# Splitting float64 weights: a parametric ReLU with slope -2^32 on ScalarE in place of a scaled copy, and one VectorE operation fewer per chunk

## Chip, cores, metric

One Trainium2 chip, one core of it. The metric is the device time of one execution in microseconds (us), as the median of several runs. Engines: PE is TensorE (matmuls), ACT is ScalarE, DVE is VectorE, POOL is GpSimd, SP issues the DMAs.

## What is computed

A chunked state-space scan over 4 sequences of 768 tokens and 8 heads, followed by two feed-forward layers of 256 x 2048 x 256. The weights arrive as numpy's float64 (`np.random.randn(...) * factor`), cut here to what matters:

```python
# scan, per batch and head, chunks of 32 tokens (L = exp of cumulated log a, causal)
y[:, :, sl] = (CB * L) @ xc + (Cc @ state) * exp(cum)
state = exp(sum(la)) * state + sum_j Bc x xc * exp(cum[-1] - cum)
# layer 1 (weights moe_w_in, moe_w_out)
h = x @ w_in;  g = np.maximum(0.01 * h, h);  x = g @ w_out
# layer 2 (weights moe2_w_in, moe2_w_out)
h = np.maximum(x @ w_in, 0.0);  out = (h * h) @ w_out
```

## The kernel before

The 3072 tokens are 12 pieces of 256 tokens, three pieces per sequence. One piece goes through the scan in two halves, `scan_a` (scales, decays, the products S of `L389` and `L390`, then `mk`) and `scan_b` (`mkh` and `mkl`, the two halves of `mk`; products Y; states `stt`; `shl`, a transpose to `t16`, four copies or DMAs into `sbd`; the second products into Y; `yh` and `yl`, the scan's result as a high and a low float32r part, or `y32` for piece 0). Layer 1 follows in blocks of one or two pieces (class `One`: `hmm` makes `hp`, `act` makes `g`, `omm` adds into `oo` or `o`), layer 2 in groups of two pieces (class `Two`). Block 0 multiplies the float32 weights as they are (`L493`, `L526`); from piece 1 on every float32 operand is split into two float32r parts and multiplied three times (`L470` to `L472`).

A weight is read in 32 chunks of 128 x 512 numbers, eight of each matrix. A chunk is loaded as 64-bit integers (`load_w`, tile `wst`) and goes through three steps, each put between other work by hand-set rules (`raw_step`, `w_one`):

- `split_w`, on ACT: `L132` scales the high 32-bit words, read as float32, by 2^-112, which rebases the exponent; `L135` scales the low words, read as unsigned integers, down to their top three bits.
- `split_w1`, on DVE: `L143` shifts the high word left by 3 and ORs the low word's bits in, which loses the sign; `L148`, `L152` or `L156` (for layer 1, `w_in` of layer 2, `w_out` of layer 2) masks the sign bit out of the unshifted high word and ORs it in. For layer 1 the result is the tile `raw`.
- `split_w2`: ACT copies to a float32r high part (`L174`), DVE subtracts it (`L175`): tiles `w1i`, `w1o`, `w2i`, `w2o`.

The text is recorded as a program first; the tile framework then orders the instructions of each engine by its own estimate of their readiness. Each engine runs its list strictly in order. So the order is no fixed text: removing an instruction can move others. DMAs all leave from SP's queue, also in order. The buffers `wst` are seven, shared with other temporary tiles such as `all` (inputs of the next sequence, read by the sums of squares `sq` of `L274`).

ACT's table of functions is loaded once, at the start (`L84`).

Of the kernel before, what the change touches and what calls it, by code (L numbers as in the profile page):

```python
# [8 lines left out]
F32 = mybir.dt.float32  # L9
# [3 lines left out]
I32 = mybir.dt.int32  # L13
I64 = mybir.dt.int64
U32 = mybir.dt.uint32
AF = mybir.ActivationFunctionType
ALU = mybir.AluOpType
# [38 lines left out]
def ssd_moe_kernel(ctx: ExitStack, tc: tile.TileContext, in1, in2, w1i, w1o, w2i, w2o, out):  # L56
# [6 lines left out]
    nc = tc.nc  # L63
# [11 lines left out]
    def big(shape, dtype, name, tag="b", bufs=None):  # L75
        return heap.tile(shape, dtype, tag=tag, name=name, bufs=bufs)
# [3 lines left out]
    ones = cp.tile([P, P], F32, name="ones")  # L80
    nc.gpsimd.memset(ones, 1.0)
    pm = cp.tile([P, 1], F32, name="pm")
    lr = cp.tile([4, 1], F32, name="lr")
    nc.scalar.activation(lr, ones[0:4, 0:1], AF.Lrelu)  # L84
    delta = cp.tile([P, U, T], F16, name="delta")


# [38 lines left out]
    def split_w():  # L126
        nm, c, st = w_loaded.pop(0)
        v = st.bitcast(I32).rearrange("p k (f two) -> p k f two", two=2)
        w0, w1 = v[:, :, :, 0], v[:, :, :, 1]


        nc.scalar.activation(w1.bitcast(F32), w1.bitcast(F32), AF.Copy, scale=2.0**-112)  # L132


        nc.scalar.activation(  # L135
            w0, w0.bitcast(U32), AF.Copy, scale=2.0**-29 * (1 - 2.0**-14), bias=7.5 * 2.0**-14 - 0.5
        )
        w_half.append((nm, c, w0, w1))

    def split_w1():  # L140

        nm, c, w0, w1 = w_half.pop(0)
        nc.vector.scalar_tensor_tensor(w0, w1, 3, w0, ALU.logical_shift_left, ALU.bitwise_or)  # L143
        if nm[0] == "1":
            if c % 2 == 0:
                pair[nm] = big([P, 2, 2, 256], F32, "raw", *RAW[nm])
            w = w_raw[nm, c] = pair[nm][:, c % 2]
            nc.vector.scalar_tensor_tensor(w.bitcast(I32), w1, -(1 << 31), w0, ALU.bitwise_and, ALU.bitwise_or)  # L148
            w_full.append((nm, c, w))
            return  # L150
        if nm != "2o":
            nc.vector.scalar_tensor_tensor(w0, w1, -(1 << 31), w0, ALU.bitwise_and, ALU.bitwise_or)  # L152
            w_full.append((nm, c, w0.bitcast(F32)))
            return
        a = big([P, 8, P], F32, "wa", "st", 7)
        nc.vector.scalar_tensor_tensor(  # L156
            a[:, 0:4].rearrange("p (k d) f -> p k (d f)", k=2).bitcast(I32),
            w1, -(1 << 31), w0, ALU.bitwise_and, ALU.bitwise_or,
        )
        nc.vector.scalar_tensor_tensor(a[:, S1], a[:, 0], -1.0, a[:, A22], ALU.mult, ALU.subtract)  # L160
        nc.vector.tensor_tensor(a[:, S3], a[:, A11], a[:, 0], ALU.subtract)
        nc.vector.scalar_tensor_tensor(a[:, S2], a[:, S1], -1.0, a[:, A11], ALU.mult, ALU.subtract)
        nc.vector.tensor_tensor(a[:, S4], a[:, A12], a[:, S2], ALU.subtract)
        w_full.append((nm, c, a[:, 1:8]))
# [12 lines left out]
    def w_step():  # L177
        if w_full:
            split_w2()
        if w_half:  # L180
            split_w1()
        if w_loaded:
            split_w()
        if wq:
            load_w()

    def raw_step():
        if w_half:
            split_w1()
        if w_loaded:  # L190
            split_w()
        if wq[0][0][0] == "1":
            load_w()

    def w_one():

        if w_full:
            split_w2()
        elif w_half:
            split_w1()  # L200
        elif w_loaded:
            split_w()
        if wq and not w_loaded:
            load_w()
# [269 lines left out]
    class One:  # L474
# [22 lines left out]
        def act(self, ms):  # L497
            n, hp = self.n * TP, self.h
            if self.f32:
                g = big([P, 512], F32, "g32", "g", 3)  # L500
                nc.scalar.activation(g, hp, AF.Lrelu)
                for j, m in enumerate(ms):
                    self.g[m] = g[:, j * n : j * n + n]
                return
            t = ap_.tile([P, 512], F32, tag="t", name="t")
            g = big([P, 2, 512], F32R, "g", "g", 3)
            nc.scalar.activation(g[:, 0], hp, AF.Lrelu)  # L507
            nc.scalar.activation(t, hp, AF.Lrelu)  # L508
            nc.vector.tensor_tensor(g[:, 1], t, g[:, 0].bitcast(F32), ALU.subtract)  # L509
            for j, m in enumerate(ms):  # L510
                self.g[m] = g[:, 0, j * n : j * n + n], g[:, 1, j * n : j * n + n]
# [289 lines left out]
```

## Time and profile before

| what | value |
|---|---|
| median of 3 runs | 606.39 us (606.07 to 607.07) |
| the profiled execution | 606.45 us |
| its span, first to last instruction | 604.7 us |
| PE busy | 572.1 us, 95% |
| DVE busy | 455.6 us, 75%, 774 instructions |
| ACT busy | 445.5 us, 74%, 715 instructions |
| DMA moved | 46.50 MB, mean 77 GB/s |

The profiled execution is 1.75 us longer than its span: what lies before the first and behind the last instruction. An engine's busy share is an average; which engine is waited for in a stretch is read from the waits and from the rows in order of time.

### The profile page before, as it was taken

The numbers are of one execution on the slowest core, as the hardware profiler recorded it, in microseconds if no ns is written. First come the engines' busy times: TensorE is split into PE (matmuls) and PEld (weight loads), VectorE is DVE, ScalarE is ACT, GpSimd is POOL, SyncE is SP. The second block draws the span as 40 slices with busy tenths as digits, with TensorE's granted clock in tenths as the row PEclk, the third lists the DMA queues.
The fourth block names the chain that finished last, engine by engine and source line by source line (L and its number), as shares of the span: only waits on it lengthen the run. The fifth ranks groups of instructions, "written<-read, shape, count | busy, mean of one in ns | idle before, by whom it ended". The sixth has DMA issues, their size and how long they took to land.

```text
span 604.7 us, 11654 instructions
## 1 busy us (share of the span) xinstructions
PE 572.1 (95%) x4610; PEld 516.3 (85%) x4610; DVE 455.6 (75%) x774; ACT 445.5 (74%) x715; POOL 5.2 (1%) x15
## 2 busy tenths in 40 slices
PE   0399999999999999999999999999999999999996
PEld 0388899999999878888888889989999999999996
DVE  6999989569984979567655468787777877877765
ACT  6999876479676868556665588877878777777773
POOL 3000000000000000000000000000000000000000
PEclk9999999999999999999999999999999999999999
DMA  8864845573576663131210000010000100100101
GB/s 295 289 160 129 234 111 116 129 193 92 113 187 189 163 166 36 36 62 46 69 36 0 1 2 0 2 36 1 9 28 1 35 1 2 36 1 0 36 1 35
DMA packets 113574, 46.50 MB, mean 77 GB/s; under 512 B 94448, under 2 KB 103280, under 8 KB 113520
## 3 DMA queue, kind: packets, MB, share of 16 engines
q1 hardware_dynamic: 113520, 45.76, 28.3%
q8 instruction: 36, 0.59, 0.4%
q14 instruction: 18, 0.15, 0.1%
HBM read 36.83 MB, written 3.15 MB: 66 GB/s over the span
## 4 chain that ended last, share of the span: by engine, by line
PE 86%; DVE 7%; ACT 4%; issue 2%; DMA 1%; DVEq 0%; ACTq 0%
PE hp L470 13%; PE hp L471 13%; PE hp L472 13%; PE o L532 4%; PE o L611 4%; PE o L538 4%; PE o L533 4%; PE o L609 4%; PE o L610 4%; PE oo L533 3%; PE oo L538 3%; PE oo L532 3%; PE Ym L611 3%; PE Ym L610 3%; PE Ym L609 3%
## 5 line engine op out<-in xcount | busy, mean ns | idle before, releaser
L509 DVE TENSOR_TENSOR g<-t,g 128x512 fp32r<-128x512 f32 x88 | 60.5, 687 | 52.6 <-ACT t L508 52.4
L587 DVE TENSOR_TENSOR tl<-ts,th 128x1024 fp32r<-128x1024 f32 x48 | 58.8, 1226 | 47.1 <-ACT th L585 47.1
L507 ACT ACTIVATE g<-hp 128x512 fp32r<-128x512 f32 x88 | 52.3, 594 | 47.2 <-PE o L538 33.7
L470 PE MATMUL hp<-yl,w1i 128*128 128x256 f32 (+1 forms) x256 | 83.4, 326 | 0.7 <-DVE yl L449 0.7
L471 PE MATMUL hp<-yh,w1i 128*128 128x256 f32 (+1 forms) x256 | 83.2, 325 | 0.0
L472 PE MATMUL hp<-yh,w1i 128*128 128x256 f32 (+1 forms) x256 | 83.0, 324 | 0.0
L575 ACT ACTIVATE b<-hp 128x512 f32<-128x512 f32 x96 | 57.2, 596 | 33.0 <-PE hp L472 32.8
L470 PE MATMUL hp<-xl,w2i 128*128 128x512 f32 x192 | 75.4, 393 | 0.0
L471 PE MATMUL hp<-xh,w2i 128*128 128x512 f32 x192 | 75.3, 392 | 0.0
L472 PE MATMUL hp<-xh,w2i 128*128 128x512 f32 x192 | 74.8, 389 | 0.0
L585 ACT CAST th<-ts 128x1024 fp32r<-128x1024 f32 x48 | 50.3, 1047 | 16.8 <-DVE ts L584 16.8
L470 PEld LDWEIGHTS hp<-yl,w1i 128*128 128x128 f32 x256 | 48.7, 190 | 4.9 <-DVE yl L449 1.1
L508 ACT ACTIVATE t<-hp 128x512 f32<-128x512 f32 x88 | 52.2, 593 | 0.0
L472 PEld LDWEIGHTS hp<-yh,w1i 128*128 128x128 f32 x256 | 48.7, 190 | 3.7
L471 PEld LDWEIGHTS hp<-yh,w1i 128*128 128x128 f32 x256 | 48.7, 190 | 3.7
L576 ACT ACTIVATE b<-b 128x1024 f32<-128x1024 f32 x48 | 50.9, 1061 | 1.1
L586 DVE TENSOR_TENSOR bl<-b,bh 128x768 fp32r<-128x768 f32 x48 | 45.7, 952 | 0.0
L582 DVE TENSOR_TENSOR ts<-b 128x512 f32<-128x512 f32 x48 | 33.2, 691 | 14.5 <-ACT b L576 13.5
L472 PEld LDWEIGHTS hp<-xh,w2i 128*128 128x128 f32 x192 | 36.1, 188 | 7.8
L470 PEld LDWEIGHTS hp<-xl,w2i 128*128 128x128 f32 x192 | 36.2, 189 | 6.3
L471 PEld LDWEIGHTS hp<-xh,w2i 128*128 128x128 f32 x192 | 36.2, 189 | 5.8
L581 ACT CAST bh<-b 128x768 fp32r<-128x768 f32 x48 | 40.1, 835 | 1.3
(167 smaller groups left out, 1571.4 us busy)
## 6 DMA issues: line engine op xcount, KB each, us to landing
in<-in SPq DMA_DIRECT2D x12, 640.0 KB, 4.9
in<-in SPq DMA_DIRECT2D x12, 512.0 KB, 5.7
all<-in SPq DMA_DIRECT2D x15, 384.0 KB, 4.3
wst<-w1i SPq DMA_DIRECT2D x8, 512.0 KB, 6.6
wst<-w1o SPq DMA_DIRECT2D x8, 512.0 KB, 6.4
wst<-w2i SPq DMA_DIRECT2D x8, 512.0 KB, 7.4
wst<-w2o SPq DMA_DIRECT2D x8, 512.0 KB, 4.2
out_t<-r SPq DMA_DIRECT2D x24, 128.0 KB, 1.7
```

What stands on the lines that cost most here:

```text
L470: nc.tensor.matmul(hp, wh[:, k, c], xl[:, :, k], start=(k == 0), stop=False)
L471: nc.tensor.matmul(hp, wh[:, k, c], xh[:, :, k], start=False, stop=False)
L472: nc.tensor.matmul(hp, wl[:, k, c], xh[:, :, k], start=False, stop=(k == KI - 1))
L507: nc.scalar.activation(g[:, 0], hp, AF.Lrelu)
L508: nc.scalar.activation(t, hp, AF.Lrelu)
L509: nc.vector.tensor_tensor(g[:, 1], t, g[:, 0].bitcast(F32), ALU.subtract)
L532: nc.tensor.matmul(self.o[d], wl[:, c], gh, start=(m == 0 and (d == 0 or self.n == 2)), stop=False, **kw)
L575: nc.scalar.activation(b[:, 2 * i : 2 * i + 2], hp.rearrange("p (n t) -> p n t", n=2), AF.Relu)
L576: nc.scalar.activation(b, b, AF.Square)
L585: nc.scalar.copy(th, t)
L586: nc.vector.tensor_tensor(bl, b[:, 1:], bh.bitcast(F32), ALU.subtract)
L587: nc.vector.tensor_tensor(tl, t, th.bitcast(F32), ALU.subtract)
```

## The change

ACT's operation on the high word becomes a parametric ReLU: a positive word is scaled by 2^-112 as before; a negative one is scaled and multiplied by -2^32 too. That makes it positive and raises its exponent by 32, which is bit 28 of the word; DVE's shift by 3 then brings that bit to place 31, the sign. So the mask operation goes, and the shift writes where the mask operation wrote. Layer 1's leaky ReLU is written as the parametric one with slope 0.01, so that it stays one function on ACT.

```diff
-    nc.scalar.activation(lr, ones[0:4, 0:1], AF.Lrelu)
+    nc.scalar.activation(lr, ones[0:4, 0:1], AF.Prelu, alpha=0.01)
...
-        nc.scalar.activation(w1.bitcast(F32), w1.bitcast(F32), AF.Copy, scale=2.0**-112)
+        nc.scalar.activation(w1.bitcast(F32), w1.bitcast(F32), AF.Prelu, scale=2.0**-112, alpha=-(2.0**32))
...
         nm, c, w0, w1 = w_half.pop(0)
-        nc.vector.scalar_tensor_tensor(w0, w1, 3, w0, ALU.logical_shift_left, ALU.bitwise_or)
         if nm[0] == "1":
...
-            nc.vector.scalar_tensor_tensor(w.bitcast(I32), w1, -(1 << 31), w0, ALU.bitwise_and, ALU.bitwise_or)
+            nc.vector.scalar_tensor_tensor(w.bitcast(I32), w1, 3, w0, ALU.logical_shift_left, ALU.bitwise_or)
...
-            nc.vector.scalar_tensor_tensor(w0, w1, -(1 << 31), w0, ALU.bitwise_and, ALU.bitwise_or)
+            nc.vector.scalar_tensor_tensor(w0, w1, 3, w0, ALU.logical_shift_left, ALU.bitwise_or)
...
-            w1, -(1 << 31), w0, ALU.bitwise_and, ALU.bitwise_or,
+            w1, 3, w0, ALU.logical_shift_left, ALU.bitwise_or,
...
-                nc.scalar.activation(g, hp, AF.Lrelu)
+                nc.scalar.activation(g, hp, AF.Prelu, alpha=0.01)
...
-            nc.scalar.activation(g[:, 0], hp, AF.Lrelu)
-            nc.scalar.activation(t, hp, AF.Lrelu)
+            nc.scalar.activation(g[:, 0], hp, AF.Prelu, alpha=0.01)
+            nc.scalar.activation(t, hp, AF.Prelu, alpha=0.01)
```

The changed text is one line shorter, so behind this place the same instruction has a line number lower by one (`L410` before is `L409` after). The built programs show three places where the order moved. In the rows a name's number tells buffers apart.

First, DVE between piece 0's `mkl` and its states `stt`. Before:

```order
L410 TENSOR_TENSOR mkl_186<-in2_111,mkh_185 128x768
L225 TENSOR_SCALAR d1e_94<-in2_164 128x16
L226 TENSOR_SCALAR in2_164<-in2_164 128x16x31
L227 MEMSET in2_164 128x16
L143 SCALAR_TENSOR_TENSOR wst_116<-wst_116 128x512
L230 SCALAR_TENSOR_TENSOR le_371<-in2_164,delta_89 128x512
L148 SCALAR_TENSOR_TENSOR raw_382<-wst_116 128x512
L337 TENSOR_SCALAR eb_339<-S_337 128x3
L143 SCALAR_TENSOR_TENSOR wst_118<-wst_118 128x512
L252 SCALAR_TENSOR_TENSOR stt_285<-dec0_95,d1s_228 128x288
```

and after:

```order
L409 TENSOR_TENSOR mkl_186<-in2_111,mkh_185 128x768
L226 MEMSET in2_164 128x16
L147 SCALAR_TENSOR_TENSOR raw_381<-wst_116 128x512
L229 SCALAR_TENSOR_TENSOR le_371<-in2_164,delta_89 128x512
L234 SCALAR_TENSOR_TENSOR le_371<-in2_164,d1e_94 128x512
L336 TENSOR_SCALAR eb_339<-S_337 128x3
L147 SCALAR_TENSOR_TENSOR raw_392<-wst_118 128x512
L251 SCALAR_TENSOR_TENSOR stt_285<-dec0_95,d1s_228 128x288
```

Of three weight operations two are left, each now writing `raw` at once; piece 1's second scan `L234` has come ahead of `stt`, and `L224` and `L225` stand ahead of `mkl`.

Second, DVE between piece 1's `mk` and its low half `mkl`. Before:

```order
L399 SCALAR_TENSOR_TENSOR in2_164<-S_454,kk_358,le_371 128x16x32
L148 SCALAR_TENSOR_TENSOR raw_636<-wst_418 128x512
L225 TENSOR_SCALAR d1e_94<-in2_374 128x16
L337 TENSOR_SCALAR eb_653<-S_649 128x3
L226 TENSOR_SCALAR in2_374<-in2_374 128x16x31
L338 TENSOR_SCALAR eb_653<-eb_653 128x3
L227 MEMSET in2_374 128x16
L143 SCALAR_TENSOR_TENSOR wst_425<-wst_425 128x512
L410 TENSOR_TENSOR mkl_453<-in2_164,mkh_452 128x768
```

and after:

```order
L398 SCALAR_TENSOR_TENSOR in2_164<-S_447,kk_358,le_371 128x16x32
L174 TENSOR_TENSOR w1i_710<-raw_381,w1i_710 128x512
L336 TENSOR_SCALAR eb_642<-S_638 128x3
L229 SCALAR_TENSOR_TENSOR le_676<-in2_374,delta_89 128x512
L337 TENSOR_SCALAR eb_642<-eb_642 128x3
L234 SCALAR_TENSOR_TENSOR le_676<-in2_374,d1e_94 128x512
L409 TENSOR_TENSOR mkl_446<-in2_164,mkh_445 128x768
```

Both scans of piece 2 (`L229`, `L234`) now stand ahead of piece 1's `mkl`; before, both stood behind it.

Third, ACT around piece 1's `yh`. Before:

```order
L174 ACTIVATE w1o_1152<-raw_557 128x512
L174 ACTIVATE w1i_1204<-raw_636 128x512
L448 ACTIVATE yh_615<-Y_502,fac_360 128x512
L274 ACTIVATE sq_689,mx_626<-all_682 128x768
L411 ACTIVATE qh_848<-le_687,sc_654 128x512
```

and after:

```order
L173 ACTIVATE w1i_1188<-raw_625 128x512
L173 ACTIVATE w1o_1191<-raw_703 128x512
L273 ACTIVATE sq_678,mx_617<-all_671 128x768
L447 ACTIVATE yh_606<-Y_495,fac_360 128x512
L410 ACTIVATE qh_832<-le_676,sc_643 128x512
```

The sum of squares `sq`, whose input `all_671` a DMA brings, has changed places with `yh`. Its DMA stands on SP behind the four DMAs into `sbd` in both programs.

## Rows read from the trace of the kernel before

**Rows 1.** The page's first part, busy us (share of the span) and instructions of TensorE.

```profile
PE 572.1 (95%) x4610; PEld 516.3 (85%) x4610; DVE 455.6 (75%) x774; ACT 445.5 (74%) x715; POOL 5.2 (1%) x15
```

**Rows 2.** Waits of TensorE: engine, line, waited for: us in total, times, longest.

```profile
PE Y L419 <- DVE mkl L410: 1.4, 2, 1.0
PE o L532 <- DVE yf L547: 1.3, 1, 1.3
PE oo L526 <- DVE raw L148: 0.9, 1, 0.9
PE hp L470 <- DVE yl L449: 0.7, 1, 0.7
```

**Rows 3.** Groups by line: busy us, mean ns | idle before, releaser.

```profile
L507 ACT ACTIVATE g<-hp 128x512 fp32r<-128x512 f32 x88 | 52.3, 594 | 47.2 <-PE o L538 33.7 <-PE hp L472 13.2
...
L132 ACT ACTIVATE wst<-wst 128x512 f32<-128x512 f32 x32 | 21.7, 679 | 3.2 <-DMA wst<-w2o 3.2
L143 DVE SCALAR_TENSOR_TENSOR wst<-wst 128x512 int32<-128x512 int32 x32 | 21.7, 686 | 2.6 <-ACT wst L135 2.5
...
L365 ACT ACTIVATE him<-in,sbp 128x512 f16<-128x512 f32 x12 | 8.7, 722 | 0.3 <-DVE sbp L344 0.2
...
L84 ACT ACT_TABLE_LOAD x1 | 1.3, 1283 | 0.7 <-PEq L791 0.7
```

**Rows 4.** VectorE in order of time, 18 to 38 us: start, us, instruction.

```profile
18.68 0.95 DVE L410 TENSOR_TENSOR mkl<-in,mkh 128x768 f16<-128x768 f32 x1
...
20.57 1.22 DVE L230 TENSOR_TENSOR_SCAN le<-in,delta 128x512 f32<-128x512 f32 x1
...
25.12 0.70 DVE L431 STREAM_TRANSPOSE t<-shl 128x512 f16<-128x512 f16 x1
...
37.08 1.29 DVE L143 SCALAR_TENSOR_TENSOR wst<-wst 128x512 int32<-128x512 int32 x2
```

**Rows 5.** ScalarE in order of time, 26 to 35 us.

```profile
26.00 1.24 ACT L355 COPY sbd<-t 32x512 f16<-32x512 f16 x2
...
29.01 0.45 ACT L444 ACTIVATE y<-Y,fac 128x256 f32<-128x256 f32 x1
...
34.19 0.60 ACT L501 ACTIVATE g<-hp 128x512 f32<-128x512 f32 x1 [1.02 <-PE hp L493]
```

**Rows 6.** TensorE in order of time, 29 to 64 us; idle before it in brackets.

```profile
29.52 8.21 PE L493 MATMUL hp<-y,raw 128*128 128x256 f32 x24 [1.16 <-ACT y L444]
...
46.55 0.19 PE L419 MATMUL Y<-mkl,xbh 128*128 128x48 f16 x1
...
58.45 1.10 PE L526 MATMUL oo<-g,raw 128*128 128x256 f32 x4 [0.88 <-DVE raw L148]
60.20 2.41 PE L526 MATMUL oo<-g,raw 128*128 128x256 f32 x10
63.31 0.39 PE L470 MATMUL hp<-yl,w1i 128*128 128x256 f32 x1 [0.71 <-DVE yl L449]
```

**Rows 7.** VectorE in order of time, 42 to 63 us.

```profile
42.44 0.75 DVE L399 SCALAR_TENSOR_TENSOR in<-S,kk,le 128x512 f32<-128x512 f32 x1 [0.40 <-PE S L390]
...
45.03 0.95 DVE L410 TENSOR_TENSOR mkl<-in,mkh 128x768 f16<-128x768 f32 x1
...
54.01 0.71 DVE L431 STREAM_TRANSPOSE t<-shl 128x512 f16<-128x512 f16 x1
...
62.51 0.75 DVE L449 SCALAR_TENSOR_TENSOR yl<-Y,fac,yh 128x512 fp32r<-128x512 f32 x1
```

**Rows 8.** In order of time, SP's queue at 57 us and ScalarE at 61 to 63 us.

```profile
57.50 0.56 SPq L315 DMA_DIRECT2D all<-in  x1
...
61.81 0.67 ACT L448 ACTIVATE yh<-Y,fac 128x512 fp32r<-128x512 f32 x1
62.38 0.83 ACT L274 ACTIVATE sq<-all 128x768 bf16<-128x768 f32 x1
```

**Rows 9.** From issue to landing of that DMA of 384 KB (line 315, at 57.5 us).

```profile
DMA to landing us min/median/max: 4.3/4.3/4.3
```

## The prediction

> **What bounds the kernel now.** I read the busy shares first: TensorE is busy for 572.1 of 604.7 us, VectorE for 75% and ScalarE for 74% [rows 1]. So a saving on VectorE counts only where TensorE waits for it. The second view is the list of TensorE's waits [rows 2]. Behind its dense work's start only four remain: 0.9 us for `raw`, 0.7 us for `yl`, 1.3 us for `yf`, and the shorter of the two waits for `mkl`, 1.4 - 1.0 = 0.4 us; 3.3 us together. The third view is each engine in order of time. Dense work starts at 29.52 us, when ScalarE's `y` is there [rows 5, 6]; the waits for `raw` and `yl` follow at 58.45 and 63.31 [rows 6]. Up to there VectorE and ScalarE run almost without a gap, feeding piece 0, piece 1 and the first weights. So the head of 63 us decides, and in it one question: when does TensorE get each thing it needs, in the new order?
>
> **The change, part by part.** *What goes:* 32 VectorE operations of 686 ns, 21.7 us, at the price of the equal form `L143` [rows 3]. Nearly all of it lies beside TensorE's work; the most that this can give are the 3.3 us of waits and an earlier start.
>
> *What is exchanged on ScalarE:* 32 scaled copies of 679 ns and 184 leaky ReLUs (88 + 88 + 8) of 594 ns become parametric ReLUs. No row shows one. From below I take no saving, since the operand sizes stay; from above the price of an operation that fetches a per-partition operand, 722 ns, so at most 0.04 us on the scaling and 0.13 us on a leaky ReLU [rows 3]. I take 0: both kinds are single passes with constants, nearest to the rows they replace.
>
> Were the parametric ReLU in another function table than the copies and squares around it, each scaling would need two loads of 1283 ns [rows 3]: 64 x 1.28 = 82 us, and the time 688 us. The built program has one load, at the start, as before; so I give this no chance.
>
> The Trainium skill, "ScalarE: Activation LUTs", section "What ACT_TABLE_LOAD costs", prices such a switch at about 2.66 us with the drain that goes with it; by that the 64 would cost 170 us (an estimate from that page). No run here shows a switch between functions.
>
> *What moves:* times below are start to start; on VectorE one 512-wide operation follows another after 0.60 us (two take 1.29, one 0.69) and a scan occupies 1.22 - 0.09 = 1.13 [rows 4]. The order is the second thing that the change alters, and I walk down it.
>
> Term 1, the start. `mkl` of piece 0 can start some 0.2 us before 18.68, when its other half `mkh` is ready. Behind it now come one `raw` (which must wait for ScalarE until 19.6), two scans and another `raw`, then `stt`: 19.63 + 0.60 + 2 x 1.13 + 0.07 + 0.60 = 23.16, 0.2 later than before. Between `stt` and the transpose stands a further `raw`, and the transpose starts at 25.44 instead of 25.12 [rows 4]. It also stands behind `L224` on piece 2's input; that DMA is asked for when `mkl` ends, 19.4, and with 4.3 us for 384 KB [rows 9], so 5.7 for its 512 KB, lands at 25.1, in time. ScalarE's share of the copies into `sbd` starts at 26.4 instead of 26.00, behind `him` and `ch`, and its `y` follows 3.0 us later as before (two copies and three operations stand between): 29.4 instead of 29.01 [rows 5]. Start of dense work: **+0.38 us**.
>
> Term 2, `mkl` of piece 1. ScalarE's first `g` slips with the start, 34.19 to 34.57, and then works without a gap through `qh`, seven weight operations, a `g` and three sums of squares, 7.2 us by their durations less 0.1 each; VectorE waits for the last weight, writes its `raw` and can start `mk` at 42.47 (42.44 before, so level). Before, `mkl` came 45.03 - 42.44 = 2.59 us later. Now stand ahead of it `mk` 0.67, `w1i` 0.60, two scans 2.26 and two small ones 0.14: 3.67, so 46.14, end 47.09 [rows 7]. TensorE comes to `L419` at 46.55 + 0.38, less one `L526` that is now behind it (two records; six more of them take 2.41 - 1.10, so 0.44): 46.49 [rows 6]. It waits until 47.15. **+0.65 us**. Queued behind this wait are `L526` and the rest of piece 1's products, so all of TensorE is late by 1.03.
>
> Term 3, the wait of 0.88 for `raw` at 58.45. VectorE's last `raw` but two now lies at 55.1 to 55.7; TensorE arrives at 58.6. The wait goes: **-0.88**.
>
> Term 4, `yl` of piece 1. From 42.47 VectorE runs through 24 more operations, 8.9 us by the same spacings, to piece 1's `stt` at 51.34, and its transpose ends at 55.05 (before 54.01 + 0.71 = 54.72) [rows 7]. SP then issues four copies and the DMA for `all`, which left 2.78 us after the transpose's end before: 57.83; it lands 4.3 us later, at 62.13 [rows 8, 9]. ScalarE would be there at 61.3 and stands before it. `sq` takes 0.82, so `yh` starts at 63.0, not 61.81; `yl` 0.70 later and TensorE 0.80 after that, as in the rows of before: 64.5 [rows 6 to 8]. TensorE is ready at 63.31 - 0.71 - 0.88 + 1.03 + 0.44 = 63.19 (one more `L526` is done by then). The wait is 1.3 instead of 0.71: **+0.60**.
>
> Term 5, the later waits for `mkl` (0.4) and `yf` (1.3). The rows between TensorE's last product and these waits are the same in number on ScalarE; on VectorE a transpose replaces a mask operation in front of `yf`. I take +0.1; both ends are small, from -0.3 (the lighter VectorE) to +0.3. Behind 215 us TensorE did not wait for VectorE for more than 0.1 us, so the rest of the saving is covered by matmuls; without that cover it would be worth up to 0.6 us a chunk.
>
> Sum: 0.38 + 0.65 - 0.88 + 0.60 + 0.1 = **+0.85 us**. Against the profiled execution that is 606.45 + 0.85 = 607.3; that execution is 0.06 above the median of the runs, so I say **607.2 us**, 0.13% above before. A change of 0.2%, 1.2 us, is about what a measurement of this kernel can tell from none.
>
> **The rivals.**
> *No net loss.* Where `all` lands before ScalarE's 61.3, term 4 falls to 0.0 or below: `yh` at 62.1, TensorE at 63.6, wait 0.4. For it: 4.3 is one landing, and the DMA engines are idle ahead of it. Against: SP sends it only after the transpose. Time: 606.3 to 606.5.
> *Faster.* The start is not late and `yl` is no longer last: if VectorE's lighter load lets the transposes of pieces 0 and 1 come early, the waits of 0.88 and 0.71 go and terms 1 and 2 are 0. It decides where `yl` ends before TensorE's 62.2. For it: sixteen VectorE operations fewer in the head, 9.6 us at 0.60. Against: the freed places are filled with scans and splits ahead of what TensorE wants. Time: 606.4 - 1.6 = 604.8.
> *A dearer parametric ReLU.* At the upper ends of the bound, seven scalings ahead of `y` cost 7 x 0.04 = 0.3; three scalings and two `g` behind that 0.1 and 0.3; then yh's queue another 0.5 at most. For it: ScalarE has no gap in the head. Against: in the blocks it idles 47 us before `g` [rows 3], so the 176 there are covered. Time: 607.2 + 1.2 = 608.4.
>
> **How the numbers follow.** Forecast 0.52, with its own range 606.6 to 607.9 (each of terms 1, 2, 4 may be off by 0.3); no net loss 0.22; faster 0.10; dearer 0.16. Below 605.2 lies the faster case: 0.10. Above 607.6 lie the dearer one and 0.3 of the forecast's: 0.16 + 0.16 = 0.32. Between: 0.58. The range from 605.7 to 608.2 leaves out the faster case and the upper part of the dearer one.
>
> **What would show it.** Dense work starting at 29.9 and not 29.5; a new wait of TensorE for `mkl` near 47 us of some 0.6; no wait for `raw` near 58; the wait for `yl` near 64 grown, with `sq` in front of `yh` released by a DMA; the `yf` wait near 212 still there. A parametric ReLU at other than 0.68 us (scaling) or 0.59 (from PSUM) would make the sum wrong, as would a DMA that lands ahead of 61.3, or a new wait in the blocks, of which the trace of before has no sign.

## The result and the profile after

The changed kernel takes 609.87 us (median of 4 runs, 609.39 to 609.95), the kernel before 606.58 us in the same session: ratio 1.0053, 95% interval 1.0035 to 1.0070, so 3.3 us slower. The forecast was 607.2 us, with a range up to 608.2. The profiled execution took 609.87 us, its span is 608.1.

The busy line of the page and the row of granted clock, 40 slices of 15.2 us; below them the row of granted clock of the kernel before (slices of 15.1 us):

```profile
PE 574.0 (94%) x4610; PEld 517.7 (85%) x4610; DVE 438.0 (72%) x742; ACT 445.8 (73%) x715; POOL 5.2 (1%) x15
...
PEclk9999899999999999999999999999999999999999
```

```profile
PEclk9999999999999999999999999999999999999999
```

VectorE lost the 32 operations and 17.6 us, ScalarE kept its time to 0.3 us [rows 1]. What is new is the 8 in the fifth slice, 61 to 76 us: TensorE did not have its full clock there.

TensorE's waits (engine, line, what it waited for: us in total, times, longest):

```profile
PE hp L469 <- DVE yl L448: 2.1, 1, 2.1
PE o L531 <- DVE yf L546: 1.3, 1, 1.3
...
PE Y L418 <- DVE mkl L409: 1.0, 2, 0.6
```

The wait for `raw` has gone, the waits for `mkl` are 0.61 and 0.35 us, `yf` is unchanged, and the wait for `yl` has grown from 0.7 to 2.1 us [rows 2]. TensorE in order of time shows where each lies, and what follows the long one:

```profile
29.89 8.36 PE L492 MATMUL hp<-y,raw 128*128 128x256 f32 x24 [1.11 <-ACT y L443]
...
47.42 0.18 PE L418 MATMUL Y<-mkl,xbh 128*128 128x48 f16 x1 [0.61 <-DVE mkl L409]
...
65.35 0.39 PE L469 MATMUL hp<-yl,w1i 128*128 128x256 f32 x1 [2.14 <-DVE yl L448]
65.57 0.28 PE L470 MATMUL hp<-yh,w1i 128*128 128x256 f32 x1
65.69 0.29 PE L471 MATMUL hp<-yh,w1i 128*128 128x256 f32 x1
...
66.93 0.41 PE L471 MATMUL hp<-yh,w1i 128*128 128x256 f32 x1
67.14 0.41 PE L469 MATMUL hp<-yl,w1i 128*128 128x256 f32 x1
67.36 0.41 PE L470 MATMUL hp<-yh,w1i 128*128 128x256 f32 x1
```

Up to 66.4 us these matmuls begin 0.12 us apart. From 66.7 to 69.7 us the same matmuls begin 0.21 us apart, with nothing to wait for. The stretches (length; PE, PEld, DVE, ACT, POOL busy; granted clock; DMA share; GB/s) say why:

```profile
64.00:66.00 2.00, 0.65 (x5) 0.65 (x6) 1.46 (x3) 2.00 (x4) 0.00 (x0) 1.00 0.95 162
66.00:68.00 2.00, 2.00 (x14) 2.00 (x14) 1.16 (x5) 1.76 (x5) 0.00 (x0) 0.64 0.12 20
68.00:70.00 2.00, 2.00 (x10) 2.00 (x10) 2.00 (x4) 0.53 (x2) 0.00 (x0) 0.51 0.93 284
70.00:72.00 2.00, 2.00 (x39) 1.75 (x38) 1.02 (x2) 1.91 (x4) 0.00 (x0) 1.00 0.97 167
```

After the idle 2.14 us the granted clock is at its lower level, 1.2 of 2.4 GHz, for (0.36 + 0.49) x 2 / 0.5 = 3.4 us. The next wait, for `mkl`, is equally long in both kernels; after and before:

```profile
98.65 0.18 PE L418 MATMUL Y<-mkl,xbh 128*128 128x48 f16 x1 [0.35 <-DVE mkl L409]
```

```profile
95.33 0.18 PE L419 MATMUL Y<-mkl,xbh 128*128 128x48 f16 x1 [0.35 <-DVE mkl L410]
```

From the matmul that waited for `yl` to this one pass 98.65 - 65.35 = 33.30 us; before, 95.33 - 63.31 = 32.02 [rows 6], with one `L526` of 0.44 more to do in it. So the half clock cost 33.30 - 32.02 + 0.44 = 1.7 us. The Trainium skill, "TensorE: Matmul & The Clock Gate", section "Terms", prices a throttled time at its length times the share of the clock that is missing: 3.4 x 0.5 = 1.7; the trace agrees.

Why `yl` is late stands on ScalarE and SP's queue, in order of time:

```profile
58.09 0.57 SPq L314 DMA_DIRECT2D all<-in  x1
...
61.02 0.64 ACT L173 ACTIVATE w1o<-raw 128x512 fp32r<-128x512 f32 x1
63.00 0.84 ACT L273 ACTIVATE sq<-all 128x768 bf16<-128x768 f32 x1 [1.34 <-DMA all<-in]
63.75 0.19 ACT L273 ACTIVATION_READ_ACCUMULATOR sq<-all 128x1 f32 x1
63.84 0.67 ACT L447 ACTIVATE yh<-Y,fac 128x512 fp32r<-128x512 f32 x1
```

`sq` stands ahead of `yh`, and ScalarE is idle for 1.34 us until the DMA of `all` has landed; before, `yh` ran at 61.81 and `sq` behind it [rows 8]. That DMA left at 58.09 us. By the list of DMA issues (KB each, us to landing) it took 4.8:

```profile
all<-in SPq DMA_DIRECT2D x1, 384.0 KB, 4.8
```

The groups by line show the price of the new operation (busy us, mean ns | idle before, what ended it):

```profile
L506 ACT ACTIVATE g<-hp 128x512 fp32r<-128x512 f32 x88 | 52.4, 595 | 48.8 <-PE o L537 34.1 <-PE hp L471 14.5
...
L132 ACT ACTIVATE wst<-wst 128x512 f32<-128x512 f32 x32 | 21.6, 674 | 3.3 <-DVE wa L162 1.7 <-DMA wst<-w2o 1.6
```

595 and 674 ns, against 594 and 679 [rows 3]. My theory A: the loss is the late `yl` (+1.4 us) and the half clock behind its wait (+1.7 us), the other terms cancelling. Against it stand B, the parametric ReLU costs something that the means hide, and C, the new order loses in many places.

### The profile page after: what moved, and what is told of

It reads as the page before. It is cut to its first block, busy times and chain, and to the rows that moved or that the text cites. A ratio compares the mean times of both kernels' runs of the same rounds, so it can differ in the third digit from the quotient of the medians.

```text
span 608.1 us, 11627 instructions
## 1 busy us (share of the span) xinstructions
PE 574.0 (94%) x4610; PEld 517.7 (85%) x4610; DVE 438.0 (72%) x742; ACT 445.8 (73%) x715; POOL 5.2 (1%) x15
## 4 chain that ended last, share of the span: by engine, by line
PE 84%; ACT 7%; DMA 3%; DVE 3%; issue 1%; SPq 1%; DVEq 0%; ACTq 0%
PE hp L469 13%; PE hp L470 13%; PE hp L471 13%; PE o L531 4%; PE o L610 4%; PE o L537 4%; PE o L532 4%; PE o L608 4%; PE o L609 4%; PE oo L531 3%; PE oo L537 3%; PE oo L532 3%; PE Ym L610 3%; PE Ym L609 3%; PE Ym L608 3%
## 5 line engine op out<-in xcount | busy, mean ns | idle before, releaser
L471 PEld LDWEIGHTS hp<-yh,w1i 128*128 128x128 f32 x256 | 49.4, 193 | 3.8
L470 PEld LDWEIGHTS hp<-yh,w1i 128*128 128x128 f32 x256 | 49.4, 193 | 3.7
```

Of the source, the lines that this page charges most:

```text
L470: nc.tensor.matmul(hp, wh[:, k, c], xh[:, :, k], start=False, stop=False)
L471: nc.tensor.matmul(hp, wl[:, k, c], xh[:, :, k], start=False, stop=(k == KI - 1))
```

## The experiments

Times are medians; a kernel is compared with the kernel before of the same session (606.11 us in the first two, 606.23 in the third). An edge is an order given to the framework by hand: what stands inside the `with` may not be issued ahead of the named instruction. A record is one instruction's entry in the trace. The last column is the lowest granted clock in any 2 us of that stretch.

| kernel | us | ratio to before, 95% interval | wait for `yl` | least clock, 62 to 72 us |
|---|---|---|---|---|
| before with the new operation alone | 605.78 | 0.9997, 0.9988 to 1.0006 | 0.74 | 1.00 |
| changed, `yh` ahead of `sq` | 606.46 | 1.0005, 0.9996 to 1.0014 | 0.73 | 1.00 |
| before, `yh` twice | 605.99 | 0.9996, 0.9987 to 1.0005 | 0.72 | 1.00 |
| changed, two edges on scans | 605.17 | 0.9990, 0.9981 to 0.9998 | 0.55 | 1.00 |
| before, `yh` five times | 609.08 | 1.0052, 1.0037 to 1.0067 | 3.71 | 0.50 |
| changed, ten useless matmuls | 610.34 | 1.0066, 1.0049 to 1.0083 | none | 1.00 |
| changed, `all` loaded earlier | 605.67 | 0.9998, 0.9978 to 1.0018 | 0.62 | 1.00 |
| changed, three edges | 605.95 | 1.0001, 0.9992 to 1.0010 | 1.10 | 1.00 |
| changed, seven useless matmuls | 609.86 | 1.0049, 1.0032 to 1.0065 | 0.39 | 1.00 |
| changed, `all` earlier, two edges | 605.32 | 0.9980, 0.9968 to 0.9992 | 0.89 | 1.00 |
| before, `all` loaded earlier | 606.32 | 1.0002, 0.9984 to 1.0019 | 0.64 | 1.00 |

### The operation alone

The sign operation stays, and the order of every engine is that of before. So that the shift does not bring a sign along, negative high words get slope 1. The leaky ReLUs are parametric ones with slope 0.01.

```diff
-        nc.scalar.activation(w1.bitcast(F32), w1.bitcast(F32), AF.Copy, scale=2.0**-112)
+        nc.scalar.activation(w1.bitcast(F32), w1.bitcast(F32), AF.Prelu, scale=2.0**-112, alpha=1.0)
...
```

> The kernel before with its weights' shift and its leaky ReLUs done as parametric ReLU, VectorE's sign operation kept, and every engine's order as before. Theory A (the loss of the change comes from piece 1's late `yl` and from the half clock that follows its wait): the instruction costs nothing, 606.6 us, with 95.3-like waits as before and the granted clock at 1.00 from 60 to 75 us. Theory B (parametric ReLU is dearer, in itself or by a table): 608 to 610 us, and a mean above 690 ns for the 128x512 shift.

605.78 us, and the scaling's mean is 681 ns. B is out: the operation costs nothing here.

### The changed kernel with `yh` ahead of `sq`

```diff
-            squares(mx[:, to : to + 1], t)
+            with tc.issue_after(last["yh", 1].ins) if s == 1 and to == 3 else nullcontext():
+                squares(mx[:, to : to + 1], t)
...
-        nc.scalar.activation(yh, Y[:, :, 0:T], AF.Copy, scale=fac)
+        last["yh", p] = nc.scalar.activation(yh, Y[:, :, 0:T], AF.Copy, scale=fac)
```

> The changed kernel with one edge more: the squares of piece 1 may not be issued ahead of `yh` of piece 1, so that ScalarE makes `yh` before `sq`, which waits for a DMA. TensorE's order is that of the changed kernel. Theory A: the wait of 2.1 us for `yl` shrinks to 0.4 to 0.7 us, the granted clock stays at 1.00 from 60 to 75 us, and the time falls by 1.5 + 1.7 = 3.2 us to about 606.6 us. Theory B (instruction price) and theory C (the loss is spread over the reordered program): 608 to 610 us. If the wait is the whole loss without the clock: 608.3 us.

606.46 us: level with before. TensorE executes the changed kernel's list. ScalarE makes `qh` and `yh` ahead of `sq` here, and on VectorE `ql` and one `w1o` have changed places with their neighbours; the rest is the same. Its wait for `yl`, from the list of TensorE's waits:

```profile
PE hp L470 <- DVE yl L449: 0.7, 1, 0.7
```

And its stretches in which the changed kernel had a clock of 0.64 and 0.51:

```profile
66.00:68.00 2.00, 2.00 (x35) 1.75 (x34) 1.76 (x3) 1.15 (x3) 0.00 (x0) 1.00 1.12 326
68.00:70.00 2.00, 2.00 (x26) 1.95 (x23) 1.75 (x3) 1.77 (x4) 0.00 (x0) 1.00 0.56 64
```

So `sq` ahead of `yh` on ScalarE held the whole loss, and C is out. It does not yet tell the wait's own 1.4 us from the clock's 1.7.

### The wait put into the kernel before, twice

```diff
+        for _ in range(1 if p == 1 else 0):
+            nc.scalar.activation(yh, Y[:, :, 0:T], AF.Copy, scale=fac)
         nc.scalar.activation(yh, Y[:, :, 0:T], AF.Copy, scale=fac)
```

> The kernel before, without any of the change, with `yh` of piece 1 made twice on ScalarE (the same operation, the same result), which puts it and `yl` behind `sq` and the DMA that `sq` waits for. Theory A: TensorE waits about 2.1 us for `yl` near 63 us instead of 0.7, the granted clock then falls to 0.5 for about 3.4 us, and the time is 606.6 + 1.4 + 1.7 = 609.7 us. If the wait does not bring the clock down: 608.0 us. Theories B and C (price of the instruction, or the new order elsewhere): at most 608.0 us, since neither is in this kernel.

605.99 us, a miss. The product that needs `yl` came 1.75 us later, as wanted, but the scheduler had seen that coming and put eight more `oo` records of 0.216 us in front; TensorE in order of time:

```profile
60.20 4.13 PE L528 MATMUL oo<-g,raw 128*128 128x256 f32 x18
65.06 0.39 PE L472 MATMUL hp<-yl,w1i 128*128 128x256 f32 x1 [0.72 <-DVE yl L451]
```

So a late `yl` costs nothing while TensorE has other work ahead of it; the test of the clock had to use that work up. The same edit with 4 for 1:

> The kernel before, without any of the change, with `yh` of piece 1 made five times on ScalarE (the same operation and result each time), so that `yl` comes about 4 us later. TensorE has five more `oo` matmuls (1.1 us) to put ahead of `yl`, and then nothing: the planned order puts a wait of 2.2 to 2.8 us there. Theory A1 (a wait of 2 us or more there brings the granted clock down for some 3 us): 0.5 in the rows of about 66 to 70 us, and 606.1 + (2.5 - 0.7) + 1.7 = 609.6 us. Theory A2 (the wait costs its own length alone): 607.9 us, clock 1.00.

609.08 us, 3.0 over before, with none of the change in it. The wait came out at 3.71 us, longer than planned, so the time alone does not decide: 3.0 us more of wait at its length alone would give 609.1 too. But the later waits and the slow first matmuls (last section) take 2.1 us less in this trace than before, which leaves room for the clock, and the clock fell, by stretches:

```profile
64.00:66.00 2.00, 0.00 (x0) 0.00 (x0) 1.45 (x5) 2.00 (x5) 0.00 (x0) 1.00 0.30 29
66.00:68.00 2.00, 0.47 (x2) 0.50 (x3) 2.00 (x5) 2.00 (x5) 0.00 (x0) 0.80 0.97 331
68.00:70.00 2.00, 2.00 (x38) 1.91 (x37) 1.54 (x3) 1.36 (x4) 0.00 (x0) 0.50 0.99 132
70.00:72.00 2.00, 2.00 (x17) 2.00 (x16) 2.00 (x3) 0.81 (x2) 0.00 (x0) 0.85 0.24 26
```

The fall of the clock belongs to the wait, not to the change.

### The wait filled with work of no use

The output does not change: the added products go into a bank of TensorE's output memory that the next matmul clears.

```diff
+            if self.p0 == 1 and ms[0] == 0:
+                for _ in range(10):
+                    nc.tensor.matmul(self.h[:, 0:TP], w_raw["1i", 0][:, 0, 0:P], y32[:, 0], start=True, stop=True)
```

> The changed kernel with ten matmuls of no use (into the `hp` bank that the next one clears) ahead of the matmul that waits for `yl`: 10 x 0.216 = 2.2 us of TensorE. ScalarE's order is the changed kernel's, so `yl` is as late; four `oo` matmuls (0.9 us) move behind. TensorE then waits 2.14 - 2.16 + 0.86 = 0.84 us. Theory A1: the clock stays at 1.00, and against the changed kernel's +3.3 us the time is +3.3 - 1.3 (idle) + 2.2 (useless work) - 1.7 (clock) = 2.5 us over the kernel before, 608.6 us. Theory A2 or C (the half clock has another cause): 0.5 again after 66 us, and +4.2 us, 610.3 us.

I had taken one such matmul for one record; it is two, so ten were 4.3 us and left no wait. 610.34 us is the time that I had given the theory with another cause, but the half clock that it needs did not come: the granted clock stayed at 1.00. With 2.2 us more work than planned the time says little by itself. With seven:

> As the kernel with ten useless matmuls, with seven. Each one of them is two records of 0.216 us in the trace (so ten were 4.3 us and left no wait at all): seven are 3.0 us, and four `oo` matmuls (1.7 us) move behind. TensorE then waits 2.14 - 3.02 + 1.73 = 0.85 us for `yl`, about as long as the kernel before does. Theory A1: clock 1.00 from 60 to 75 us, and over the kernel before 3.3 - 1.3 + 3.0 - 1.7 = 3.3 us, plus up to 1 us of later waits as with ten: 609.4 to 610.4 us. Theory A2 (the half clock is not the wait's): 0.5 in the rows after 66 us, 611 us or more.

609.86 us. ScalarE still has `sq` ahead of `yh`, but TensorE's list of waits has only this for `yl`:

```profile
PE hp L469 <- DVE yl L448: 0.4, 1, 0.4
```

And its clock stays up, by stretches:

```profile
66.00:68.00 2.00, 2.00 (x23) 1.70 (x22) 2.00 (x6) 1.27 (x3) 0.00 (x0) 1.00 0.91 281
68.00:70.00 2.00, 2.00 (x38) 2.00 (x35) 1.97 (x4) 1.48 (x3) 0.00 (x0) 1.00 0.98 168
```

Against the changed kernel's trace the last wait (0.12 us, for layer 2) comes 0.8 us earlier, at 601.07 for 601.87 us, though TensorE does 3.0 us more. The other differences are 1.75 less of this wait, 0.2 less of the waits behind it, a start 0.2 later and three slow matmuls fewer at the start, 0.6 (last section): +0.6 without the clock, -1.1 with its 1.7 us. -0.8 is close to the second. So 3.0 us of useless work cost next to nothing, since it kept the clock up: each in its own session, 3.6 us over before with it and 3.3 without.

All thirteen traces agree on the price of the clock. From the end of TensorE's last matmul I take the start of the dense work, TensorE's waits from there on, what the slow first matmuls take beyond 0.216 us each, and the useless work, all from its rows in order of time. What is left is 564.4 us in the kernel before and 564.1 to 564.8 in the ten other traces in which the clock stayed up; it is 566.15 in the changed kernel and 565.9 with `yh` five times, 1.7 and 1.5 more than before.

### The transfer asked for earlier

```diff
-        for to, at in ((0, N + T), (3, N + T + 16), (1, N), (4, N + 16), (2, 0)):
...
+        def load_all(at):
             t = big([P, NPC, U * 16], F32, "all", "st", 7)
             nc.sync.dma_start(t, all_[:, :, U * at : U * (at + 16)])
+            ld.append(t)
...
+        load_all(ats[0][1])
+        for i, (to, _) in enumerate(ats):
+            if i < 4:
+                load_all(ats[i + 1][1])
             yield
-            squares(mx[:, to : to + 1], t)
+            squares(mx[:, to : to + 1], ld[i])
```

> The changed kernel with each of the five loads of `all` issued one step earlier (one load ahead of the squares that need it). No edge is put on ScalarE, but the plan then has `yh` of piece 1 ahead of the `sq` behind it. Theory A: `sq` no longer holds up `yh`; the wait for `yl` is 0.4 to 0.9 us, the clock 1.00 from 60 to 75 us, 606 to 607 us. Theory C (the loss is spread over the reordered program): 608 us or more.

605.67 us: the loss is gone here too, with the framework's planned order itself putting `yh` first; one of the ten runs took 610.8 us all the same (last section). And the same edit on the kernel before:

> Control: the kernel before, sign operation and all, with the loads of `all` one step earlier. Theory A: nothing waits for these loads in the kernel before in front of `yl` (`yh` stands ahead of `sq`), so the time is that of before, 606.1 us, within 0.5 us. If the early loads are a gain of their own, with or without the change: 605.5 us or less.

606.32 us. The early load is no gain of its own; it only undoes the changed kernel's defect.

### Orders that might beat both

First, piece 2's scans behind piece 1's `mkl`, and piece 1's start scan behind piece 0's `stt`:

```diff
+        with tc.issue_after(last["mkl", 1].ins) if p == 2 else nullcontext():
             lt, e1 = decays(az)
...
+        with tc.issue_after(last["stt", 0].ins) if p == 1 else nullcontext():
             from_start(p, az, e1)
```

> The changed kernel with two edges more: the scans of piece 2 come behind `mkl` of piece 1, and piece 1's start behind piece 0's `stt`; in the order that results ScalarE also makes `yh` of piece 1 ahead of `sq`. Theory A: the later start (+0.4) and the wait near 47 us (+0.6) go, the wait for `raw` (0.9) stays away, the wait for `yl` is 0.4 to 0.7 us and the granted clock stays at 1.00 from 60 to 75 us: about 605.5 us. Theory B: 608 us or more. Theory C (the reordered program loses elsewhere): 607 us or more.

605.17 us, 0.9 under before. The wait for `mkl` near 47 us went, but the dense work started at 30.97 us: the scan, let go behind `stt`, still stood ahead of the `sbd` chain. With the edge on the `sbd` copies instead, and `yh` ahead of `sq`:

> The changed kernel with three edges: piece 1's start scan behind piece 0's `sbd` copies, piece 2's scans behind piece 1's `mkl`, and the squares of the second sequence behind `yh` of piece 1. Theory A with the terms of the forecast: the dense work starts near 28.9 us (0.6 ahead of before, since `stt` and the `sbd` chain have VectorE to themselves), no wait near 47 us, no wait for `raw` (0.9), the wait for `yl` at 0.4 to 0.7 us: 606.1 - 1.5 = 604.6 us. If the gain of the removed sign operations is lost elsewhere: 606 us.

605.95 us, no gain. The start came at 29.20 us and the waits for `raw` near 58 us and for `mkl` near 47 us went, as asked, but the wait for `yl` grew to 1.10: `yl` ended no earlier than before, so part of what was saved ahead of it was waited out there. Part of the earlier start was lost at once, too. The third weight load of TensorE (PEld) had to wait for VectorE's half of `y`, which the same view of the kernel before does not show:

```profile
30.50 0.50 PEld L496 LDWEIGHTS hp<-y,raw 128*128 128x128 f32 x2 [0.79 <-DVE y L448]
```

Last, the two edges with the early load:

> The changed kernel with the loads of `all` one step earlier and two edges (piece 1's start scan behind piece 0's `sbd` copies, piece 2's scans behind piece 1's `mkl`). If the terms of the forecast add up: start at 29.2 us, no wait near 47 us and none for `raw`, 0.6 us for `yl`: 605.2 us, at best with the kernel that has only the two scans moved. If what is saved ahead of `yl` is given back in the wait for it (as in the kernel with three edges): 606.0 us.

605.32 us, 0.9 us under the kernel before, as with the first two edges. Its ratio of 0.9980 (0.9968 to 0.9992) looks better than theirs because three of the runs of the kernel before that it is compared with took over 608 us (last section). From its list of TensorE's waits:

```profile
PE hp L504 <- ACT y L455: 1.1, 1, 1.1
PE hp L481 <- DVE yl L460: 0.9, 1, 0.9
...
PE o L543 <- DVE yf L558: 0.4, 1, 0.4
```

Of these three versions the two that gain have a shorter wait for `yf` (0.41 and 0.14 us), and the one that doesn't has 1.24. The last one has the late half of `y` as well (0.80 us), so that alone does not part them. I did not test either wait by itself, so where their 0.9 us lies stays open.

## Why the prediction was wrong

| term | forecast | measured |
|---|---|---|
| 1, start of dense work | +0.38 | +0.37 |
| 2, `mkl` of piece 1 | +0.65 | +0.61 |
| 3, `raw` at 58 us | -0.88 | -0.88 |
| 4, `yl` of piece 1 | +0.60 | +1.43 |
| 5, later waits | +0.1 | -0.05 |
| clock behind the wait for `yl` | not in the sum | +1.7 |
| sum | +0.85 | +3.2, of 3.4 between the two profiled executions |

Terms 1, 2, 3 and 5 held, and so did their mechanism. The changed kernel with `yh` first has just these terms and is level with before: 0.37 + 0.61 - 0.88 is nothing much. Most of what is missing between 3.2 and 3.4 is 0.15 us more of slow first matmuls (last section), which no term had.

**Term 4 was mis-sized.** The place and the mechanism, `sq` in front of `yh` behind a DMA, were right. TensorE was ready at 65.35 - 2.14 = 63.21 us, where I had 63.19. But I had the DMA leave at 57.83 and land 4.3 us later, from one landing [rows 9]; it left at 58.09 and took 4.8, so `sq` began at 63.00 and not at 62.13. In the trace of the kernel before the fifteen loads of `all` took from 3.7 to 8.0 us, so the spread was there to be read. I gave this term 0.3 either way, and it was off by 0.83. That alone would have made 607.2 + 0.83 = 608.0 us, still inside the range.

**The step that failed** is the last sentence of term 4: "The wait is 1.3 instead of 0.71", priced at the difference. A longer wait of the engine that bounds the kernel was priced at its length alone. The runs show that at 2.14 us it also takes TensorE's clock down, for another 1.7 us (and at 3.71, in the kernel before, for another 1.5). With the wait at 0.73 the clock stays up, and the kernel is level with before. No term, and none of the rivals, had this in it, so the range ended at 608.2.

Of the rivals, the dearer parametric ReLU is out by its own price and by the kernel with the operation alone. "No net loss" is what the changed kernel becomes once `yh` is first: its condition, `all` landing before 61.3 us, was the right question, and the DMA answered it by 1.6 us the wrong way. "Faster" needed edges that the change does not bring, and even with them 605.2 us was the best.

## What to carry to other kernels

Where a scheduler decides the order, removing work on an engine that is not waited for may buy nothing by itself, as here, and the new order may put an instruction that waits for a DMA ahead of one that the bounding engine needs; look for that pair first, and give the transfer its spread, not its one measured landing. Price a wait of TensorE in the midst of dense work by its length only as long as traces have waits of that length, there, that left the granted clock alone; beyond, add the stretch at half clock. And before testing with a late operand, count the matmuls that the scheduler can put ahead of it.

## What the runs showed that I had not expected

Waits of TensorE in the midst of dense work of 1.30 us (for `yf`, before), 1.25 (after) and 1.10 us left the granted clock at 1.00, and so did one of 1.65 us for `yf` in the kernel with ten useless matmuls:

```profile
PE o L534 <- DVE yf L549: 1.7, 1, 1.7
```

2.14 and 3.71 us brought it to 0.5; between 1.65 and 2.14 nothing was measured.

All four runs of the changed kernel took over 609.3 us, at a mean clock of 0.995 or 0.996; the eleven runs with `yh` put ahead of `sq` are at 0.998 to 1.000. (A mean of 0.997 alone tells nothing: the traces show the lower level behind the last matmul too, for up to 3.2 us of the span.) The kernel before now and then comes near the changed one: 3 of 24 in the last session took 608.3 to 608.5 us at a mean clock of 0.996. With `all` loaded earlier, one run of the changed kernel took 610.8 and one of the kernel before 611.0, at 0.996 and 0.994. There is no trace of those, so it is not shown that a late `yl` was behind them.

The first matmuls of the dense work begin 0.43 us apart and later ones 0.22, at a granted clock that reads 1.00 throughout. In the changed kernel, by stretches:

```profile
32.00:34.00 2.00, 2.00 (x6) 1.53 (x6) 1.51 (x3) 1.76 (x5) 0.00 (x0) 1.00 0.88 124
34.00:36.00 2.00, 2.00 (x7) 1.60 (x6) 1.05 (x2) 2.00 (x5) 0.00 (x0) 1.00 0.36 41
36.00:38.00 2.00, 2.00 (x11) 1.77 (x10) 0.99 (x2) 2.00 (x6) 0.00 (x0) 1.00 0.41 47
```

Six matmuls in 2 us, then eleven, counting those that reach in from outside. The number of slow ones differs between executions, from some 6 to 12 in the profiled ones (11 and a partly slow one in the kernel before, 12 and one in the changed kernel), and each costs 0.21 us. That is up to 1.3 us between two executions, of the size of the spread of the runs of before (605.1 to 606.9 us in the first two sessions). What sets the number was not tested. 0.43 to 0.22 is about the ratio of the two levels of the clock, and TensorE idled for 5.1 us or longer until 27 to 29 us in every trace; but the granted clock reads 1.00 through all of that, so whether it was down there is not shown.
